# First batch of a Fourier filter and MLP mixer: filter requests moved to an earlier stage and to one queue, its real part doubled on chip, mixer input read in two parts

## The chip, the cores and the metric

The kernel runs on one core of a Trainium2 chip. The metric is the device time of one execution in microseconds (us). Executions of one program mostly agree within 0.3%. A "ratio" below is the mean time of one kernel's fast runs over that of the other's of the same rounds, so it is not quite the ratio of the medians quoted beside it. Where one run's profile is compared with another's, the times are those of the profiled execution.

## The reference

A filter in the frequency domain, then an MLP mixer, all float32 apart from the 64-bit weights.

```python
# x: (8, 3008, 256); filt_r, filt_i: (1505, 256)
X = np.fft.rfft(x, axis=1)
y = np.fft.irfft(X * (filt_r + 1j * filt_i)[None], n=3008, axis=1).astype(np.float32)
xt = y.transpose(0, 2, 1)
h  = np.maximum(xt @ w_tok1, 0.0) @ w_tok2        # token MLP, 256 hidden, 64-bit weights
u  = y + h.transpose(0, 2, 1)
out = (u + np.maximum(u @ w_ch1, 0.0) @ w_ch2).astype(np.float32)   # channel MLP, 1536 hidden
```

## The kernel before

The transform of length 3008 = 64 x 47 is done as matmuls in two stages. The length-64 stage reads x, multiplies, and stores the result z in HBM (`z_tmp`). The filter stage goes through 32 "residues", in 16 pairs: it reads a pair's rows of z, multiplies them with a table `wb` on TensorE, multiplies the result with the filter on VectorE (three products a residue), transforms back on TensorE, lets ScalarE copy the result out of the accumulator into a buffer `t3`, and stores it in HBM as g (`g_tmp`). The mixer then reads g as `t4` in six pieces. Only the first of the five groups of batches does this with no mixer of another batch beside it. During it SP also loads the 64-bit weights w1 and GpSimd w2, and VectorE converts them in `convert()` steps, twelve pieces of w1 and sixteen of w2, the last of them after the filter stage has ended.

What the change and the argument touch, with cuts marked by `# ...`:

```python
def filt_load(c, queues):              # a pair's filter: real part twice (both halves of the rows), imaginary once
    t, k0 = filts[c % FB], c * KC      # FB = 3 buffers
    for q, (src, i, p0) in zip(queues, ((filt_r, 0, 0), (filt_r, 0, HALF), (filt_i, 1, HALF))):
        q.dma_start(t[p0:p0 + A, i], raw(src, k0, [[64 * D, A], [D, KC], [1, D]]))
        # ... two more pieces of 16 and 7 rows
# ...
def load(c):                           # in dft(bs)
    # ... wb of the pair: nc.sync.dma_start(wbs[g], ...)
    filt_load(c, (nc.sync, nc.gpsimd, nc.gpsimd) if first else (nc.sync,) * 3)
    # ... z of the pair: nc.sync.dma_start(t2s[c], z_d ...)
# ...
def bi_unit(k):
    # ... matmuls back; t3 has two buffers; ScalarE copies the accumulator into it
    if r == KC - 1:
        # ...
        nc.scalar.dma_start(g_d[b, ts(c, KC)]..., t3[:, :, i, :])
load(0)
load(1)
yield
yield
for k in range(K2 + 1):
    if k < K2:
        b_unit(k)
        if k % KC == 0 and k // KC + 2 < K2 // KC:
            load(k // KC + 2)
    if k >= 1:
        bi_unit(k - 1)
    yield
# ...
def t4_load(b, c):
    t4[b, c] = t4p.tile([P, TC4, D], FP32, tag="t4", name="t4")
    nc.sync.dma_start(t4[b, c], rows_of(g_d, b)[:, ts(c, TC4), :])
```

`nc.sync` is the queue of SyncE (SP), `nc.gpsimd` that of GpSimd, `nc.scalar` that of ScalarE (ACT). One point of the built program, which the source does not show: the transfers that SP and ACT issue use eight completion counters in turn, and each transfer is issued only once the one eight before it has landed. The traces record it: the transfers of these two queues signal eight semaphores in turn, 100, 101, 110 to 113, 115 and 116.

## Time and profile before

| | kernel before |
|---|---|
| median | 2620.95 us (3 runs, 2620.94 to 2629.69) |
| profiled span | 2619.4 us |
| VectorE's first filter product | 48.24 us |
| from it to the first product of residue 28 | 75.84 us |
| from there to the end of the last w2 conversion | 47.95 us |
| end of the last w2 conversion, when the mixer starts | 172.03 us |
| from there to the end | 2447.4 us |

The marks are read from VectorE's timeline. From the fourth of the forty slices on TensorE is at 90% or more in all but the last, so a microsecond won before 172.03 us is won at the end unless something later takes it back. The lines themselves stand in the prediction.

### The profile page before, as it was taken

What the parts mean: (1) busy time and instruction counts of PE and PEld (TensorE: products, weight loads), DVE (VectorE), ACT (ScalarE), POOL (GpSimd) and SP (SyncE); (2) the same over time, 40 slices, a digit from 0 to 9 for tenths busy, and PEclk for the clock granted to TensorE, in tenths of its full rate; (3) what the DMA queues carried; (4) which work ended last, traced back from release to release, by engine and by line L of the source; (5) the groups of instructions that cost most, each with busy time, mean ns of one, the idle gap of its engine ahead of it and who ended that gap; (6) DMA issues with size and microseconds to landing.
All of it is one profiled execution on the core that took longest, in us unless ns stands there. A gap on an engine that the chain in (4) does not pass through costs nothing.

```text
span 2619.4 us, 31533 instructions
## 1 busy us (share of the span) xinstructions
PE 2513.3 (96%) x10928; PEld 2000.7 (76%) x10928; DVE 1804.4 (69%) x3461; ACT 678.9 (26%) x1325; POOL 519.3 (20%) x951
## 2 busy tenths in 40 slices
PE   6869999999999999999999999999999999999998
PEld 2446666788878777888787777788888888888887
DVE  3787788645666888646567688745678586647676
ACT  2223222222321222213222222212222122212222
POOL 3534111211121111211212111121121121211212
PEclk7879999999999999999999999999999999999999
DMA  8765433312232332202332222211322111100001
GB/s 235 221 192 177 123 111 111 103 42 89 85 100 63 88 89 61 87 9 90 95 101 85 74 82 75 75 33 56 95 77 84 54 46 55 25 9 8 17 10 22
DMA packets 158104, 212.89 MB, mean 81 GB/s; under 512 B 35012, under 2 KB 106383, under 8 KB 157945
## 3 DMA queue, kind: packets, MB, share of 16 engines
q1 hardware_dynamic: 85897, 120.34, 15.7%
q0 software_dynamic: 30656, 39.92, 6.2%
q10 hardware_dynamic: 41392, 50.62, 5.7%
q8 instruction: 86, 1.41, 0.2%
q14 instruction: 73, 0.60, 0.1%
HBM read 135.77 MB, written 74.97 MB: 80 GB/s over the span
## 4 chain that ended last, share of the span: by engine, by line
PE 74%; DVE 14%; issue 2%; ACT 1%; DMA 0%; DVEq 0%; SPq 0%; POOL 0%; ACTq 0%; POOLq 0%
PE ps_po L562 26%; PE ps_pg L528 15%; PE ps_pg L544 11%; PE ps_acc L488 6%; PE ps_acc L471 6%; PE ps_acc L493 3%; DVE t L506 3%; DVE hh L506 3%; PE ps_b L410 3%; PE ps_b L378 2%; PE ps_acc L434 2%; DVE u L506 2%; DVE s L506 1%; DVE p L425 1%; DVE p L424 1%
## 5 line engine op out<-in xcount | busy, mean ns | idle before, releaser
L506 DVE TENSOR_TENSOR hh<-ps_pg,s 128x512 f32<-128x512 f32 (+3 forms) x864 | 482.8, 586 | 643.8 <-ACT s L531 643.2
L607 POOL DMA_DIRECT2D out_dram<-r x757 | 409.8, 550 | 1964.7 <-ACT hh L549 893.9
L549 ACT ACTIVATE hh<-hh 128x512 f32<-128x512 f32 (+1 forms) x576 | 348.0, 621 | 1103.0 <-DVE hh L506 1103.0
L562 PE MATMUL ps_po<-t,wc 128*128 128x256 f32 (+1 forms) x2304 | 535.5, 375 | 3.5 <-DVE t L506 2.2
L562 PEld LDWEIGHTS ps_po<-t,wc 128*128 128x128 f32 x2304 | 434.4, 190 | 127.6 <-issue 50.8
L562 PE MATMUL ps_po<-hh,wc 128*128 128x256 f32 (+1 forms) x1728 | 413.1, 375 | 3.1 <-ACT hh L549 3.1
L528 PE MATMUL ps_pg<-v,wc 128*128 128x256 f32 (+1 forms) x1728 | 414.1, 376 | 1.6 <-DVE v L506 1.6
L562 PEld LDWEIGHTS ps_po<-hh,wc 128*128 128x128 f32 x1728 | 327.4, 190 | 42.4 <-ACT hh L549 5.1
L528 PEld LDWEIGHTS ps_pg<-v,wc 128*128 128x128 f32 x1728 | 327.6, 190 | 41.7 <-DVE v L506 2.3
L544 PE MATMUL ps_pg<-u,wc 128*128 128x256 f32 (+1 forms) x1152 | 294.1, 378 | 9.6 <-DVE hh L506 9.3
L506 DVE TENSOR_TENSOR t<-t,hh 128x256 f32<-128x256 f32 (+1 forms) x576 | 242.9, 422 | 19.8
L544 PEld LDWEIGHTS ps_pg<-u,wc 128*128 128x128 f32 x1152 | 215.3, 190 | 49.2 <-DVE hh L506 22.3
L506 DVE TENSOR_TENSOR s<-ps_pg,hh 128x512 f32<-128x512 f32 (+1 forms) x288 | 196.1, 681 | 30.6 <-DVE hh L506 0.5
L506 DVE TENSOR_TENSOR t<-hh 128x512 f32<-128x512 f32 (+1 forms) x288 | 192.5, 668 | 0.6 <-ACT hh L549 0.6
L488 PE MATMUL ps_acc<-w,h 128*128 128x512 f32 (+1 forms) x384 | 181.7, 596 | 7.7 <-ACT h L477 3.5
L471 PE MATMUL ps_acc<-t,w 128*128 128x256 f32 x768 | 170.3, 384 | 8.0 <-DMA t<-g_tmp 6.7
L528 PE MATMUL ps_pg<-u,wc 128*128 128x256 f32 (+1 forms) x576 | 170.3, 377 | 0.4 <-DVE hh L506 0.4
L471 PEld LDWEIGHTS ps_acc<-t,w 128*128 128x128 f32 x768 | 147.5, 193 | 29.8 <-issue 7.1
L544 PE MATMUL ps_pg<-v,wc 128*128 128x256 f32 (+1 forms) x576 | 168.9, 375 | 0.0
L410 PE MATMUL ps_b<-t,wb 96*128 96x512 f32 (+1 forms) x288 | 130.3, 533 | 31.8 <-DMA t<-z_tmp 17.6
L434 PE MATMUL ps_acc<-p,wb 128*96 128x256 f32 (+1 forms) x384 | 154.7, 497 | 2.4 <-DVE p L423 1.1
L531 ACT COPY s<-ps_pg 128x256 f32<-128x256 f32 (+1 forms) x288 | 106.0, 368 | 152.0 <-PE ps_pg L528 147.4
(71 smaller groups left out, 1954.2 us busy)
## 6 DMA issues: line engine op xcount, KB each, us to landing
z_tmp<-t ACTq DMA_DIRECT2D x96, 256.0 KB
t<-z_tmp SPq DMA_DIRECT2D x128, 192.0 KB
g_tmp<-t ACTq DMA_DIRECT2D x128, 192.0 KB
t<-g_tmp SPq DMA_DIRECT2D x48, 512.0 KB
x<-in_x_dram SPq DMA_DIRECT2D x184, 128.0 KB
out_dram<-r POOLq DMA_DIRECT2D x698, 32.0 KB, 1.8
wb<-wbi_t SPq DMA_DIRECT2D x80, 224.0 KB
filt<-in_filt_r_dram SPq DMA_DIRECT2D x144, 48.0 KB
```

Source lines behind the costliest of these rows:

```text
L410: nc.tensor.matmul(ps, wbs[k // WC][0:KR, k % WC, 0:P], t2s[k // KC][:, k % KC], start=True, stop=True)
L434: nc.tensor.matmul(ps[0:KR], wbs[k // WC][:, k % WC, P:], p, start=(i == 0), stop=(i == len(parts) - 1))
L471: nc.tensor.matmul(acc[:, t, :], w1[:, a, ts(t, P)], t4[b, a // TC4][:, a % TC4, :], start=(a == 0 and t == 0), stop=(a == A - 1 and t == ...
L488: nc.tensor.matmul(ps[:, 0:w], h1[:, t, ts(dh, P)], w2[:, t, ds(m * 512, w)], start=(t == 0), stop=False)
L493: nc.tensor.matmul(ps[:, ds(q * P, n)], t4[b, c][:, r, ts(dh, P)], wai[:, 0:n], start=False, stop=(q == 3))
L506: nc.vector.tensor_tensor(out=out, in0=in0, in1=in1, op=op)
L528: nc.tensor.matmul(ps[:, 0:hw], wc1[:, jp, n, :], mov, start=True, stop=True)
L531: nc.scalar.copy(out=s[:, 0], in_=g[0][:, 0, 0:hw])
L544: nc.tensor.matmul(ps[:, 0:hw], wc1[:, jp, n, :], mov, start=True, stop=True)
L549: nc.scalar.activation(out=hs, in_=hs, func=AF.Relu)
L562: nc.tensor.matmul(po[i][:, j, 0:hw], wc2[:, jp, n, :], mov, start=(jp == 0 and first == 1), stop=(jp == JP - 1 and last == 1))
L607: q.dma_start(rows[g, e, :, ds(h * A + 4 * m, n)], blocks[ts(g, CW), h, e, 0:n])
```

## The change

Its intent is to take waits for transfers out of the first batch, where nothing hides them. It has three parts: (1) the filter of the first batch is asked for by GpSimd alone, its real part once instead of twice, and ScalarE copies that to the other half of the rows; (2) in the first batch, the first two pairs' filter and wb are asked for during the length-64 stage, and in all groups the z rows are asked for before wb; (3) rows 0 to 95 of the first batch's mixer input, which hold residues 0 to 23, are asked for during the last six steps of the filter stage, and the rest after it.

```diff
+LAST_STEP = NXC + 2 + K2
+EARLY_ROWS = 96
-    def filt_load(c, queues):
+    def filt_load(c, first):
         t, k0 = filts[c % FB], c * KC
-        for q, (src, i, p0) in zip(queues, ((filt_r, 0, 0), (filt_r, 0, HALF), (filt_i, 1, HALF))):
+        q = nc.gpsimd if first else nc.sync
+        for src, i, p0 in ((filt_r, 0, 0), (filt_i, 1, HALF)) + (() if first else ((filt_r, 0, HALF),)):
 # ...
+    def filt_double(c):
+        t = filts[c % FB]
+        nc.scalar.copy(out=t[HALF:P, 0], in_=t[0:HALF, 0])
 # ... w_load(c): wb on nc.sync, then filt_load(c, first)
         for i, u in enumerate(todo):             # the length-64 stage
+            if first and i in (5, 8):
+                w_load(i // 6)
 # ...
-        load(0)
-        load(1)
+        for c in range(2):
+            t2_load(c)
+            if not first:
+                w_load(c)
         yield
         yield
+        if first:
+            filt_double(0)
         for k in range(K2 + 1):
             if k < K2:
                 b_unit(k)
                 if k % KC == 0 and k // KC + 2 < K2 // KC:
-                    load(k // KC + 2)
+                    t2_load(k // KC + 2)
+                    w_load(k // KC + 2)
+                if first and k % KC == KC - 1 and k + 1 < K2:
+                    filt_double(k // KC + 1)
 # ...
-    def t4_load(b, c):
+    def t4_load(b, c, lo=0, hi=P):
 # ... in the main loop, from the length-64 stage's end on:
+                if LAST_STEP - 6 <= i < LAST_STEP:
+                    t4_load(0, i - LAST_STEP + 6, 0, EARLY_ROWS)
 # ... after the stage:
-            t4_load(0, c)
+            t4_load(0, c, EARLY_ROWS)
```

## The prediction

> **What bounds the kernel now.** I began with the page's busy table and its forty slices, to see which part of the kernel the change can touch at all.
>
> ```profile
> PE 2513.3 (96%) x10928; PEld 2000.7 (76%) x10928; DVE 1804.4 (69%) x3461; ACT 678.9 (26%) x1325; POOL 519.3 (20%) x951
> ...
> PE   6869999999999999999999999999999999999998
> DVE  3787788645666888646567688745678586647676
> PEclk7879999999999999999999999999999999999999
> ```
>
> A slice is 65.5 us. TensorE is full from the fourth slice on, so after the first batch's filter nothing but less TensorE work would help, and the change removes none: the built programs of both kernels have the same matmuls in the same order, and the same VectorE list. What can be won lies in the first three slices. In the timeline the first matmul of the mixer proper (L528) starts at 181.10 us. Two per cent of 2620.95 is 52 us, and no reordering takes 52 of these 181 us away, as the sums below show; so the answer is "within 2%" from the start, and the question is how many microseconds.
>
> Next I read the same stretch in the timeline of each engine: the length-64 stage is 0 to 38 us, the filter stage (L410 to L439) 47 to 134 us, the mixer's weights, token sums and first inputs up to 181 us. Windows over the last two (first line: columns):
>
> ```profile
> core 0: us, PE busy (x) PEld busy (x) DVE busy (x) ACT busy (x) POOL busy (x), PEclk, DMA share, GB/s
> 48.20:133.10 84.90, 71.94 (x234) 41.84 (x232) 65.70 (x145) 23.86 (x53) 48.07 (x87) 0.91 0.78 214
> 133.10:172.00 38.90, 26.51 (x101) 20.83 (x101) 36.97 (x85) 9.77 (x18) 13.25 (x25) 0.80 0.80 255
> ```
>
> From 133 to 172 us VectorE is busy 37.0 of 38.9 us, and the rest is the few hundredths between instructions: it converts the weights w2 without a pause. The end of that stretch shows who waits for whom:
>
> ```profile
> 140.51 23.76 PE L471 MATMUL ps_acc<-t,w 128*128 128x256 f32 x96 [6.74 <-DMA t<-g_tmp]
> 167.78 2.07 PE L488 MATMUL ps_acc<-w,h 128*128 128x512 f32 x2 [3.51 <-ACT h L477]
> 172.00 2.08 PE L488 MATMUL ps_acc<-w,h 128*128 128x512 f32 x2 [2.14 <-DVE w L242]
> ...
> 171.17 0.86 DVE L242 TENSOR_TENSOR w<-both 128x368 f32<-128x368 f32 x2
> ```
>
> TensorE waits 6.74 us for the mixer input, but its token sums are ready at 164.3 us and their relu at 167.7 us; what starts the mixer at 172.0 us is VectorE's last w2 conversion. So VectorE carries the path from the filter stage's end, and a gain must shorten the filter stage as VectorE sees it. There VectorE is busy 65.7 of 84.9 us. The gaps that its timeline lists there (larger than the 0.03 us between any two) add up to 0.78 + 2.83 + 1.25 + 0.71 + 0.20 + 1.68 + 4.06 + 1.44 + 0.20 + 1.64 + 0.94 = 15.7 us. They start at TensorE, which waits for the z rows:
>
> ```profile
> 68.10 1.19 PE L410 MATMUL ps_b<-t,wb 96*128 96x256 f32 x2 [2.70 <-DMA t<-z_tmp]
> 69.08 1.91 PE L434 MATMUL ps_acc<-p,wb 128*96 128x256 f32 x4
> ...
> 96.46 1.22 PE L410 MATMUL ps_b<-t,wb 96*128 96x256 f32 x2 [3.41 <-DMA t<-z_tmp]
> ```
>
> and those rows come late because their request stands in the SP queue behind other things. The waits of that queue from 38 to 137 us:
>
> ```profile
> SPq L401 <- PE ps_acc L434: 21.3, 11, 3.9
> SPq L465 <- DMA g_tmp<-t: 15.0, 2, 7.8
> SPq L193 <- DMA g_tmp<-t: 9.0, 2, 5.0
> SPq L406 <- DMA g_tmp<-t: 6.6, 2, 4.8
> ```
>
> L401 (the table wb) waits 21.3 us for a free buffer, with the z request behind it. L193 and L406 (filter, z) wait 15.6 us for g_tmp, which they don't read: in the built program the transfers of SP and ACT share eight completion counters in turn, so each waits for the one eight before it. With wb, three filter pieces and z, one store of g and 1.33 w1 pieces for two residues (7.3 transfers), eight back is the previous pair's g store, just issued.
>
> **The Trainium skill.** "DMA: Bandwidth & Descriptors", section "Anatomy of one DMA": most of a transfer's fixed time is the receipt of the write, heaviest when the target is HBM. This trace agrees: the stores of g are what the SP queue waits for, up to 5.0 us at L193. Its "Rules for kernel authors" say that several issuing queues save only issue time, as the same 16 engines move all; so giving the filter to GpSimd wins no bandwidth, and only the bytes dropped count. "TensorE: Matmul & The Clock Gate", section "What's actually happening": after an idle window of about 3.4 us the array runs at half clock until it has been busy as long. Here too: the four-instruction group L434 takes 1.91 us at 69.08 and 1.03 us at 76.08; so a z wait costs again after it (the gaps of 1.25, 0.71 and 1.44 us). "ScalarE: Activation LUTs", section "What ACT_TABLE_LOAD costs": 186 ns + 0.833 ns per column, 613 ns for 512; L256's copies of 512 columns took 0.59 us.
>
> **The change part by part.**
> Removed: SP's 3 filter pieces for each pair of residues, of 24 + 23 rows of two 1 KB packets. That is 15 x 94 = 1410 packets in the filter stage, 55 ns each on the trace (mean of that queue's 1 KB packets), over 16 engines 4.8 us of 0.78 x 84.9 = 66 us of DMA time. GpSimd issues as many pieces as before; its first three groups are asked for by 14.2 us in both kernels, since nothing in its queue holds them.
> Moved: the z request ahead of wb, so it no longer waits for L434 or the filter. Per pair 4.3 transfers on the eight counters instead of 7.3, so eight back is nearly two pairs old, some 8 us at VectorE's pace, longer than the 5 us seen. I expect the six waits for z (0.78 + 2.83 + 1.68 + 4.06 + 1.64 + 0.94 = 11.9 us of VectorE's gaps) and their half-clock echoes (3.4 us) to go for the greater part.
> VectorE's pace sets what is left: three residues take 9 x 0.445 us for the products and 2.26 us for a w1 conversion, 6.26 us; TensorE needs 6.14 us for the same (75.65 to 81.79), so the two are nearly level and a hiccup of either is paid.
> Added: 16 copies of 64 x 512 on ScalarE, 0.59 us each, 9.4 us of an engine busy 23.9 of 84.9 us. Most fit in its 1.19 us pauses between two evacuations L439. In five of the 16 places (the step after a w1 conversion, an even one) the copy falls between L214 and an evacuation with only 0.13 us free (L214 ends 58.53, L439 starts 58.66), which delays it by 0.45 us; the acc bank is single, so TensorE pays: 5 x 0.45 = 2.3 us. The copies also need the filter's real part a step before VectorE did; GpSimd's pieces land 3.8 us after issue and are asked for some 8 us ahead. I leave 2.5 us for copies or z rows that still come late, with the stage compressed.
> Stage: 15.7 - 2.3 - 2.5 = about 11 us.
> The start: two wb (128 packets of 107 ns each on 16 engines, 0.86 us) go into the length-64 stage, where the DMA share reaches 1.0; that may cost up to 1.7 us. In return z is asked for as soon as the last z store lands (SP waited for that until 43.21 and asked at 44.32): 1.1 us won. Net +0.5 us lost.
> The mixer input in two parts: three quarters arrive before the stage ends, so TensorE's 6.74 us shrink to perhaps 3. All of it is behind VectorE, which already binds by 172.0 - 167.7 = 4.3 us: worth 0.
> The later batches only reorder requests; there L410's waits (14.0 us) are for VectorE, not for transfers: 0.
> Sum: 2620.95 - 11 + 0.5 = 2610.5, say 2611.
>
> **Rivals.** (a) Transfers bind by volume: the stage keeps its DMA-limited length and gains only the 4.8 us removed: 2616. For it: DMA share 0.78 with 1.0 in places; against: 61 us of DMA work fit in 74. (b) The doubling becomes the new wait: ScalarE stands in order behind a late filter, evacuations slip, and 16 x 0.6 us come back: 2620. For it: TensorE and VectorE are level, GpSimd also carries w2 in the second half (landing 5.3 us); against: the pauses of ScalarE. (c) The early mixer input is worth its 3.7 us too, because something ties w2 to it: 2607. Against it: VectorE's unbroken conversions. (d) The start loses more than I think: wb delays the last x, all moves by 3 us: 2613.
>
> **Range and chances.** The stage's gain lies between 4 and 15.7 us, start and rest within 2 us; two of the three times of before agree to 0.01 us, one is 8.7 us off. Range 2603 to 2619. Faster or slower by 2% needs 52 us either way: 0.01 each.
>
> **What would show it.** In the changed profile: the waits of L410 for z under 5 us in all; the span from VectorE's first product to its last under 76 us (84.8 before); copies of 0.59 us and few evacuations waiting behind them; VectorE still without pauses up to the last w2 conversion, now near 161 us, and TensorE still waiting for it; the token sums' wait shorter without effect. I am wrong if the z waits stay, if ScalarE waits for the filter by microseconds, or if w2's end moves by a different amount than the last product.

## The result, and the profile after

The changed kernel took 2618.26 us (median of 4 runs, 2615.93 to 2619.16), the kernel before 2621.26 us in the same rounds (4 runs, 2620.94 to 2629.69): ratio 0.9979, with a 95% interval of 0.9959 to 1.0. The range and the class "within 2%" held, but the range by 0.7 us only, and one of the four runs (2619.16 us, the profiled one) lies above it; the centre, 2611 us, was 7 us too low. The profile says which terms of the sum were wrong. First its page (busy table and slices):

```profile
PE 2510.9 (96%) x10928; PEld 2000.0 (76%) x10928; DVE 1804.1 (69%) x3461; ACT 688.5 (26%) x1341; POOL 518.9 (20%) x951
...
PE   5869999999999999999999999999999999999998
DVE  3887788646666788646567788745678586647676
...
PEclk7989999999999999999999999999999999999999
```

The work is what it was; ScalarE alone has 16 instructions and 9.6 us more, which are the copies. Only the first three slices can differ, so the same marks are compared:

| us | first product | to residue 28 | to end of w2 | w2 ends | rest | span |
|---|---|---|---|---|---|---|
| before | 48.24 | 75.84 | 47.95 | 172.03 | 2447.4 | 2619.4 |
| changed | 50.83 | 62.57 | 54.32 | 167.72 | 2449.7 | 2617.4 |
| difference | +2.59 | -13.27 | +6.37 | -4.31 | +2.3 | -2.0 |

So the stage up to residue 28 gained 13.3 us, as much as was hoped for; the start lost 2.6 us, and the stretch behind residue 28 lost 6.4 us. The mixer starts 4.3 us earlier, and 2.3 us of that do not reach the end of this profiled run: TensorE had two more half-clock stretches after the mixer's start (near 204 and 870 us) than the kernel before. A repeat of the changed kernel (e0 below) had neither and a rest of 2446.6 us, so this is variation between runs and not the change.

The windows of the changed kernel (columns as in the prediction's windows: stretch, its length, busy time of TensorE, weight loads, VectorE, ScalarE and GpSimd, granted clock, DMA share, GB/s):

```profile
50.80:113.00 62.20, 59.04 (x207) 34.57 (x207) 57.14 (x125) 29.76 (x61) 47.45 (x85) 0.98 0.87 237
113.00:131.00 18.00, 10.42 (x28) 5.36 (x26) 10.78 (x26) 3.68 (x9) 1.61 (x3) 0.83 0.90 260
131.00:168.00 37.00, 24.79 (x99) 20.00 (x100) 34.63 (x79) 9.29 (x17) 12.51 (x24) 0.82 0.67 185
```

Up to 113 us VectorE and TensorE are both above 90% busy and the clock is 0.98; in the kernel before it was 0.91 over the whole stage. Then come 18 us in which VectorE is busy only 10.8, with the DMA share at 0.90, the highest of the three.

The waits of the SP queue from 38 to 140 us (line, what it waited for: total us, times, longest):

```profile
SPq L401 <- PE ps_acc L448: 34.0, 13, 3.7
SPq L487 <- DMA g_tmp<-t: 18.6, 1, 18.6
SPq L420 <- PE ps_pg L424: 8.6, 5, 4.4
SPq L420 <- DMA z_tmp<-t: 7.0, 1, 7.0
```

The waits of z and filter for g stores (L406 and L193 before) are gone. What is left for g_tmp is L487, the second part of the mixer input, which really needs the last g store. The 7.0 us for z_tmp are the first z request, before the stage.

TensorE's timeline (start, duration, instruction; in brackets the idle time before it and what ended it):

```profile
49.54 1.19 PE L424 MATMUL ps_b<-t,wb 96*128 96x256 f32 x2 [9.05 <-DMA t<-z_tmp]
...
135.47 22.40 PE L493 MATMUL ps_acc<-t,w 128*128 128x256 f32 x96 [5.31 <-DMA t<-g_tmp]
...
163.52 2.07 PE L510 MATMUL ps_acc<-w,h 128*128 128x512 f32 x2 [5.65 <-ACT h L499]
...
167.69 2.08 PE L510 MATMUL ps_acc<-w,h 128*128 128x512 f32 x2 [2.10 <-DVE w L250]
```

The wait of 9.05 us for z is the one that opens the stage; inside it no wait for z is left. At the end the mixer still starts on VectorE's last w2 conversion (L250), so a loss on VectorE's path is a loss in the time.

The loss itself stands in the timelines of ScalarE and VectorE. ScalarE:

```profile
113.83 0.31 ACTq L458 DMA_DIRECT2D g_tmp<-t  x1
115.75 0.62 ACT L202 COPY filt<-filt 64x512 f32<-64x512 f32 x1 [1.95 <-DMA filt<-in_filt_r_dram]
117.19 0.37 ACT L453 COPY t<-ps_acc 96x256 f32<-96x256 f32 x1 [0.82 <-DMA g_tmp<-t]
...
127.72 0.37 ACT L453 COPY t<-ps_acc 96x256 f32<-96x256 f32 x1 [4.51 <-DMA g_tmp<-t]
```

VectorE:

```profile
119.73 0.43 DVE L438 SCALAR_TENSOR_TENSOR p<-ps_b,filt 64x256 f32<-64x256 f32 x1 [2.91 <-DMA filt<-in_filt_i_dram]
...
131.58 0.36 DVE L224 TENSOR_SCALAR both<-both 128x376 uint32<-128x376 uint32 x1 [4.03 <-ACT both L222]
```

L453 writes a `t3` buffer, of which there are two, and each waits for the store that last used it. The store issued at 113.83 us is the one that the evacuation at 127.72 us waits for, so it took about 13.9 us; the one issued at 109.26 us held the evacuation at 117.19 us, some 7.9 us. The evacuation at 127.72 us stands in ScalarE's order before the step of the w2 conversion that is ScalarE's (L222), and so VectorE stands idle for 4.03 us although the weight itself has nothing to do with g. The filter pieces come late too: 1.95 us ahead of a copy, 2.91 us ahead of a product. SP had asked for the first early part of the mixer input at 109.38 us.

### The profile page after: what moved, and what is told of

Read it like the earlier page. It is cut to its first block, busy times and chain, and to the rows that moved or that the text cites. A ratio compares the mean times of both kernels' runs of the same rounds, so it can differ in the third digit from the quotient of the medians.

```text
span 2617.4 us, 31439 instructions
## 1 busy us (share of the span) xinstructions
PE 2510.9 (96%) x10928; PEld 2000.0 (76%) x10928; DVE 1804.1 (69%) x3461; ACT 688.5 (26%) x1341; POOL 518.9 (20%) x951
## 4 chain that ended last, share of the span: by engine, by line
PE 74%; DVE 14%; issue 2%; ACT 1%; DMA 1%; DVEq 0%; SPq 0%; POOL 0%; ACTq 0%; POOLq 0%
PE ps_po L584 26%; PE ps_pg L550 15%; PE ps_pg L566 11%; PE ps_acc L510 6%; PE ps_acc L493 6%; PE ps_acc L515 3%; DVE hh L528 3%; DVE t L528 3%; PE ps_b L424 3%; PE ps_b L386 2%; PE ps_acc L448 2%; DVE u L528 2%; DVE s L528 2%; DVE p L439 1%; DVE p L438 1%
## 5 line engine op out<-in xcount | busy, mean ns | idle before, releaser
L448 PE MATMUL ps_acc<-p,wb 128*96 128x256 f32 (+1 forms) x384 | 154.5, 496 | 10.5 <-ACT t L453 8.6
```

The lines of the kernel that those rows point to most:

```text
L448: nc.tensor.matmul(ps[0:KR], wbs[k // WC][:, k % WC, P:], p, start=(i == 0), stop=(i == len(parts) - 1))
```

## The experiments

The theory after the result: the gain comes from the filter's transfers that no longer stand among the eight counters (and perhaps from z going ahead of wb), and the early read of 2.36 MB (six parts of 384 KB) delays the last g stores and filter pieces. One rival for the lost time (B) was that the shorter stage lets GpSimd's w2 loads, 376 KB each, fall on the last residues whatever the mixer input does. Another (C) was that TensorE's own chain, the token sums, had become the bound, so that the early read could not hurt or help. Nine runs were made. Runs of the kernel before: median 2623.2 us (9 runs) for e1, e2, e4 and e6, 2620.55 us (7 runs) for e0, e3, e5 and e8, and 2624.15 us (7 runs) for e9. All outputs were correct.

| us | first product | to residue 28 | to end of w2 | w2 ends | rest | median | ratio to before |
|---|---|---|---|---|---|---|---|
| e0 changed again | 51.64 | 62.52 | 51.91 | 166.07 | 2446.6 | 2614.66 | 0.9978 [0.9963, 0.9993] |
| e1 one read | 50.28 | 63.54 | 47.05 | 160.87 | 2446.1 | 2608.89 | 0.9947 [0.9935, 0.9960] |
| e2 early read only | 49.35 | 75.16 | 53.07 | 177.58 | 2448.5 | 2625.63 | 1.0010 [0.9997, 1.0024] |
| e6 early read of 48 rows | 48.90 | 62.11 | 50.61 | 161.62 | 2447.2 | 2611.53 | 0.9956 [0.9943, 0.9970] |
| e4 no doubling | 51.86 | 72.85 | 47.24 | 171.95 | 2446.4 | 2619.21 | 0.9986 [0.9971, 1.0002] |
| e3 wb late | 47.44 | 62.27 | 47.00 | 156.71 | 2447.9 | 2608.20 | 0.9953 [0.9938, 0.9968] |
| e5 doubling only | 47.47 | 62.47 | 47.12 | 157.06 | 2448.7 | 2607.16 | 0.9949 [0.9932, 0.9965] |
| e8 early read, 1 KB packets | 47.41 | 62.48 | 51.27 | 161.16 | 2447.3 | 2612.40 | 0.9969 [0.9954, 0.9984] |
| e9 doubling, tiny transfers | 47.31 | 75.35 | 49.68 | 172.34 | 2449.2 | 2623.15 | 0.9991 [0.9968, 1.0014] |

### e1: the mixer input in one read

```diff
-                if LAST_STEP - 6 <= i < LAST_STEP:
-                    t4_load(0, i - LAST_STEP + 6, 0, EARLY_ROWS)
 # ...
-            t4_load(0, c, EARLY_ROWS)
+            t4_load(0, c)
```

> The changed kernel with the mixer input read in one part again, after the last residue. Marks on VectorE's timeline: first product (before 48.2, changed 50.8 us), first product of residue 28 (124.1, 113.4), end of the last w2 conversion (172.0, 167.7); the tail from residue 28 to that end grew from 48.0 to 54.3 us in the changed kernel. Theory A: the early read fills the DMA engines while the last g stores and filter pieces need them. Then the tail falls back to about 48 us, the last w2 conversion ends near 161.4 us, and the time is some 6 us under the changed kernel, about 2612 us. Rival B: the crowd is GpSimd's four w2 loads, which come in a bunch because the stage is faster; then the tail stays at 54 us and the time near 2618 us. Rival C: the later mixer input makes TensorE's token sums the end of the path; then the w2 conversions end near 161 us, but the mixer's first input starts microseconds after that.

The stretch behind residue 28 fell from 54.32 us (51.91 in e0) to 47.05, and the median of the run to 2608.89 us. The same stretch of time as in the changed kernel's second window, and then TensorE's timeline:

```profile
113.00:131.00 18.00, 9.87 (x34) 5.63 (x33) 17.09 (x40) 6.60 (x15) 2.68 (x5) 0.81 0.68 220
```

```profile
129.47 23.42 PE L493 MATMUL ps_acc<-t,w 128*128 128x256 f32 x96 [6.83 <-DMA t<-g_tmp]
...
160.84 2.08 PE L510 MATMUL ps_acc<-w,h 128*128 128x512 f32 x2 [2.10 <-DVE w L250]
```

VectorE is busy 17.1 of the 18 us instead of 10.8, and the DMA share is 0.68 instead of 0.90. ScalarE shows no wait for a g store between 104 and 124 us. Three w2 loads are asked for in a bunch here too, from 111.1 to 113.5 us (111.4 to 113.1 in the changed kernel), but they land in 4.4 to 4.7 us instead of 10.5 to 14.5, so rival B falls. TensorE waits longer for its input than before the removal (6.83 us against 5.31), and still starts the mixer on VectorE's conversion, 6.85 us earlier: rival C falls. The times agree: the ratios to the kernel before of e1 (0.9935 to 0.9960) and of the changed kernel's repeat e0 (0.9963 to 0.9993) do not overlap.

### e2: the early read alone, in the kernel before

```diff
 # kernel before, plus LAST_STEP, EARLY_ROWS and t4_load(b, c, lo, hi)
+                if LAST_STEP - 6 <= i < LAST_STEP:
+                    t4_load(0, i - LAST_STEP + 6, 0, EARLY_ROWS)
 # ...
-            t4_load(0, c)
+            t4_load(0, c, EARLY_ROWS)
```

> The kernel before with only the mixer input read in two parts. Theory A: the same crowding in a slower stage; the tail grows from 48.0 us by 3 to 6 us, the time to 2624 to 2627 us, and the shorter wait of the token sums wins nothing. Rival B (w2 loads): tail 48 us, time 2621 us as before. My prediction's step (the early read is worth 0) would also give 2621 us.

```profile
177.56 2.07 PE L491 MATMUL ps_acc<-w,h 128*128 128x512 f32 x2 [2.11 <-DVE w L244]
```

The stretch behind residue 28 grew by 5.1 us (53.07 against 47.95), and the mixer started 5.6 us later, again on VectorE's conversion. VectorE again had a gap of 4.99 us behind ScalarE's step of the conversion (at 141.51 us). The medians differ by 2.4 us only, and the interval just includes 1, so the time alone would not prove the cost; the trace shows it, and it is there without any other part of the change.

### e6: half the rows early

```diff
-EARLY_ROWS = 96
+EARLY_ROWS = 48
```

> The changed kernel with 48 instead of 96 rows read early (half the bytes, asked at the same places). Theory A: the excess of the tail over 48.0 us halves, from 6.4 to about 3 us; time about 2615 us. Rival B: the tail stays at 54 us. A third theory, that a g store waits on the completion counter of an early read rather than for the engines' bandwidth, would leave the tail nearly as it is, since the number of transfers is unchanged.

The stretch took 50.61 us. Over the 47.05 of e1 that is 3.6 us, where 96 rows cost 4.9 (e0) and 7.3 us (the first profile). Half the bytes cost less, but not clearly half. ScalarE still waited 3.64 us for a g store. The third theory of the expectation, a g store held by the completion counter of an early read, does not apply here: in the changed kernel, e0 and e6 each g store of this stretch was issued within 0.03 us of the end of its evacuation.

### e4: no doubling, the order and the early requests kept

```diff
 # e1, and:
-        for src, i, p0 in ((filt_r, 0, 0), (filt_i, 1, HALF)) + (() if first else ((filt_r, 0, HALF),)):
+        for src, i, p0 in ((filt_r, 0, 0), (filt_i, 1, HALF), (filt_r, 0, HALF)):
+            if first and (i, p0) == (0, HALF):
+                q = nc.sync
 # ... both calls of filt_double removed
```

> As e1_one_read, but no doubling: the real part's second copy is loaded by SP behind wb, as three pieces, the z request still first. It tells what of the 13.3 us won between the first product and residue 28 (75.8 to 62.6 us) is the order of the requests and what is the doubling with its fewer transfers. My prediction's reading (both matter: order frees z from wb's wait, fewer transfers age the eight counters): 66 to 70 us. If order alone is enough: 63 us or less, as ScalarE's copies go too. If the number of transfers on the shared counters is what counts: 72 us or more, with waits of the SP queue for g stores back.

```profile
79.53 1.19 PE L426 MATMUL ps_b<-t,wb 96*128 96x256 f32 x2 [2.93 <-DMA wb<-wbi_t]
```

```profile
81.32 0.43 DVE L439 TENSOR_TENSOR p<-ps_b,filt 128x256 f32<-128x256 f32 x1 [4.10 <-DMA filt<-in_filt_r_dram]
...
99.24 0.42 DVE L439 TENSOR_TENSOR p<-ps_b,filt 128x256 f32<-128x256 f32 x1 [3.64 <-DMA filt<-in_filt_r_dram]
```

The stage to residue 28 took 72.85 us: 10 of the 13 us are gone. Of the outcomes named beforehand it was the third and not the prediction's reading (66 to 70 us), and SP's waits for g stores are back (8.6 us at L403, wb). With z first, the waits did not vanish; they moved to whatever now came last in the queue, wb and the filter's real part. The order is worth 3 us at most when the filter stays on SP.

### e0: the changed kernel again

No edit.

> The changed kernel again, on another chip perhaps, to tell what of its marks repeats. It ended 2449.7 us after its last w2 conversion, the kernel before 2447.4 and e1_one_read 2446.1, with two more half-clock windows on TensorE late in the trace (near 204 and 870 us). If those are chance, that stretch comes to 2446 to 2448 us this time; if they belong to the change, to 2449 us or more. The tail from residue 28 to the last w2 conversion should be about 54 us again (theory A).

The median was 2614.66 us against 2620.55 us for the kernel before, ratio 0.9978. The marks vary: 51.91 us behind residue 28 instead of 54.32, and a rest of 2446.6 us instead of 2449.7. Differences of 2 or 3 us between two single profiles carry no argument here.

### e3: wb asked for late

```diff
 # e1, and wb split off w_load as wb_load:
             if first and i in (5, 8):
-                w_load(i // 6)
+                filt_load(i // 6, first)
 # ...
         for c in range(2):
             t2_load(c)
+            wb_load(c)
             if not first:
-                w_load(c)
+                filt_load(c, first)
```

> As e1_one_read, but the first two wb are asked for behind the z requests, not in the length-64 stage. The first product came at 48.2 us before, at 50.8 and 50.3 us with wb early, but also at 48.9 (wb early) and 49.4 (wb late) in others. If the early wb delays the last z store (my prediction: up to 1.7 us), the first product comes 1 to 2 us sooner than 50.3 us, near 49 us, and the time is 1 to 2 us under e1_one_read. If wb behind z is itself waited for, the first product stays at 50 us or later and nothing is won.

The first product came at 47.44 us instead of 50.28, and the stage was as short as before. Single profiles vary, so all of them are taken: the six kernels with wb in the length-64 stage have first products at 50.83, 51.64, 50.28, 51.86, 48.90 and 47.41 us, on average 50.15; the five others at 48.24, 49.35, 47.44, 47.47 and 47.31 us, on average 47.96. With the early wb the first product is about 2.2 us later on average, but with a spread of 4 us among the six, and the lowest of them (47.41, e8) is as early as the others. The times do not confirm a cost: as ratios to the kernel before, e3 (0.9953) and e5 (0.9949, wb late too) do not differ from e1 (0.9947). It was run at another time. That the early wb costs time is not shown.

### e5: the doubling alone

```diff
 # kernel before, and:
-    for q, (src, i, p0) in zip(queues, ((filt_r, 0, 0), (filt_r, 0, HALF), (filt_i, 1, HALF))):
+    parts = ((filt_r, 0, 0), (filt_i, 1, HALF)) if queues is None else (... the three of before)
+    for q, (src, i, p0) in zip(queues or (nc.gpsimd,) * 2, parts):
 # ...
-    filt_load(c, (nc.sync, nc.gpsimd, nc.gpsimd) if first else (nc.sync,) * 3)
+    filt_load(c, None if first else (nc.sync,) * 3)
 # ... filt_double called where the changed kernel calls it; wb still before z, one read of the mixer input
```

> The kernel before with the doubling alone: SP asks for no filter, but wb still stands before z and is asked for after the length-64 stage. e4_no_double showed that the order alone leaves 72.8 us from the first product to residue 28 (75.8 before, 62.6 to 63.5 with both). If the number of transfers on the eight shared counters is the cause of the waits, the doubling alone brings 63 to 65 us and a time within 3 us of e1_one_read. If z must also be ahead of wb's wait for its buffer, it brings 67 to 71 us, with waits of TensorE for z left.

The waits of its SP queue from 47 to 125 us (a third entry, 0.4 us for the w2 conversion, is not shown):

```profile
SPq L406 <- PE ps_acc L439: 41.8, 13, 7.3
SPq L474 <- DMA g_tmp<-t: 15.0, 3, 8.3
```

The whole gain of the stage is there, 62.47 us to residue 28, although z still stands behind wb, which waits 41.8 us for its free buffer (L406). VectorE's gaps after the first product come to 1.70 us, where the kernel before had 15.7. Only the mixer input (L474) waits for g stores now; neither filter nor z waits for another transfer. The median, 2607.16 us, is the best of all, 7.5 us below the changed kernel.

### e8: the early read in 1 KB packets

```diff
 # changed kernel; the early part of t4_load becomes
+            for h in range(2):
+                nc.sync.dma_start(t4[b, c][lo:hi, h::2], src[:, h::2, :])
```

> The changed kernel with each early read as two transfers of alternate rows: the same bytes in packets of 1 KB instead of 4 KB. If the engines take turns between queues by packets, a g store (1 KB packets) loses less to each turn, and the tail's excess over 48 us falls from 6.4 to 3 to 5 us. If only the bytes count, it stays at 6 us; if the twelve transfers instead of six weigh on the eight counters, it grows.

If the DMA engines took turns between queues by packet, smaller packets of the read should have let the g stores through. The stretch took 51.27 us, against 51.91 in e0 and 54.32 in the first profile: within what two runs of one kernel differ by. The trace says more than this sum, for the wait is another one. ScalarE:

```profile
113.51 0.37 ACT L453 COPY t<-ps_acc 96x256 f32<-96x256 f32 x1 [1.19 <-PE ps_acc L448]
119.91 0.31 ACTq L458 DMA_DIRECT2D g_tmp<-t  x1
120.26 0.58 ACT L264 COPY w<-ps_po 128x512 f32<-128x512 f32 x1 [6.38 <-DMA t<-g_tmp]
```

No evacuation waits for a `t3` buffer any more: the store issued at 110.31 us had nearly all its packets moved from 115 to 118 us, where that of 113.83 us in the changed kernel needed from 118 to 127.7 us. But the next store, due at 113.88 us, was issued only at 119.91 us, when the completion counter that it shares with the early read of 108.29 us came free. The smaller packets may have eased one wait, and the six transfers more brought another; what the packets alone are worth stays open.

### e9: the doubling, with three tiny transfers a pair put back

```diff
 # e5, and in load(c), before the z request:
+    if first:
+        for n in range(3):
+            nc.sync.dma_start(idle[0:A, (3 * c + n) % 16, :], raw(filt_r, c * KC + n, [[64 * D, A], [1, 8]]))
```

> e5_double_only plus three tiny loads (24 rows of 32 bytes, never read) on the SP queue where the three filter pieces stood: the count of transfers is that of the kernel before, the bytes are those of the doubling. The stretch from the first product to residue 28 was 75.8 us before and 62.5 us with the doubling alone. If the count on the eight shared completion counters is the cause, most of the 13.3 us comes back: 70 to 76 us, with waits of the SP queue for g stores and of TensorE for z. If the bytes and packets of the filter pieces are the cause, it stays at 62 to 64 us.

Each of the three brings 24 rows of 32 bytes into a tile that nothing reads: the count of the removed transfers without their bytes. Its SP queue's waits from 47 to 125 us, and TensorE's waits:

```profile
SPq L407 <- PE ps_acc L443: 23.6, 8, 4.6
SPq L411 <- DMA g_tmp<-t: 4.1, 3, 2.2
SPq L407 <- DMA g_tmp<-t: 3.2, 2, 2.9
SPq L407 <- DMA st<-in_moe_w_tok_dram: 1.8, 2, 1.3
```

```profile
75.53 0.70 PE L419 MATMUL ps_b<-t,wb 96*128 96x256 f32 x2 [1.88 <-DMA t<-z_tmp]
...
92.38 0.70 PE L419 MATMUL ps_b<-t,wb 96*128 96x256 f32 x2 [2.34 <-DMA t<-z_tmp]
...
109.81 0.70 PE L419 MATMUL ps_b<-t,wb 96*128 96x256 f32 x2 [2.94 <-DMA t<-z_tmp]
```

The stage is back at 75.35 us (75.84 in the kernel before), and wb (L407) and the tiny loads (L411) wait for g stores that they do not read. All waits of this queue for transfers that the request does not need sum to 14.2 us. So the gain was neither bytes nor order but the number of transfers on the shared counters. Two reservations: the tiny loads also take about 1 us of SP's issue time a pair, and one of the four timed runs was at 2614.28 us where the others lay from 2623.03 to 2626.38 us, which I cannot explain.

## Why the prediction was right or wrong

**The bound, and the class: right.** All of it happened in the first 170 us, the mixer started on VectorE's last w2 conversion in every trace in which I looked at it, and 52 us were out of reach.

**The stage's gain, predicted 11 us from first to last product: right in mechanism, and conservative.** First to last product went from 84.8 to 73.9 us (50.83 to 124.70), under the predicted 76; without the early read it was 71.6 us (e1), a gain of 13.2. The step "4.3 transfers on the eight counters instead of 7.3" is what e5 and e9 confirm: doubling alone gives 62.47 us to residue 28, three tiny transfers a pair give 75.35. The other half of that step, "the z request ahead of wb", is not needed: e5 has the old order and loses nothing. What the prediction held back for copies and late rows, 2.3 and 2.5 us, was about 1.9 us of gaps on VectorE up to residue 28 (0.46 + 0.36 + 0.85 + 0.24). The hiccups are where it put them, at five steps after a conversion, about 0.55 us each on TensorE. The copies took 0.62 us, not the 0.59 of L256; the figures that the prediction takes from "ScalarE: Activation LUTs" are those of an ACTIVATE with immediate scale and bias, and give an estimate of 0.61 us for 512 columns.

**The start, predicted +0.5 us: mis-sized.** It was +2.6 in the profile and about 2.2 on average over the traces. The prediction gave wb up to 1.7 us and took back 1.1 us for an earlier z request. That credit did not come: SP waited for the last z store until 46.60 us, not until 43.21, because the last store of the length-64 stage landed later. That the early wb is what delayed this store was not shown (e3).

**The failed step: "The mixer input in two parts ... worth 0".** This is where the centre was lost. The prediction asked only who waits for the mixer input (TensorE, with slack behind VectorE), and that was right: TensorE's wait shrank from 6.74 to 5.31 us without effect. It did not ask what the early 2.36 MB would delay. They were sent when the last g stores, filter pieces and w2 loads were also under way; the store of 113.83 us kept one of the two `t3` buffers for 13.9 us, ScalarE stood behind it, and with it the w2 conversion that sets the mixer's start. In the changed kernel this cost 4.9 to 7.3 us (e0 and the first profile against e1), in the kernel before 5.1 us (e2). With 5 to 7 us here and 1.7 to 2.1 us at the start, less the 2.2 us more that the stage gave once freed of it (13.2 against 11), the centre of 2611 becomes 2615.5 to 2617.9 us; the two calls gave 2618.26 and 2614.66.

**The rivals of the prediction.** (a) Volume: fell, as e9 gives back nearly the whole gain with 2.3 KB a pair (3 x 24 x 32 bytes). (b) The doubling as a new wait: fell for the stage; one copy waited 1.95 us for its filter at 115.75 us, in the stretch crowded by the early read. (c) The early input is worth 3.7 us: the opposite. (d) A costly start: partly right. That GpSimd's queue brings no bandwidth, which the prediction takes from "Rules for kernel authors", no run here tests.

**Still open.** How the early read holds up the g stores is settled in part. ScalarE's queue moved no data from 116 to 118 us, although the store of 113.83 us was waiting; no run gives a reason. From 118 us on this store shared the engines with the early read and the w2 loads. What each queue moved from 119 to 124 us in the changed kernel (packets, MB, share of the engines' time; q0 is GpSimd's queue, q1 SP's, q10 ScalarE's):

```profile
q0 software_dynamic: 159, 0.76, 50.0%
q1 hardware_dynamic: 169, 0.60, 37.9%
q10 hardware_dynamic: 160, 0.16, 13.3%
```

The three moved nearly the same number of packets, but those of the w2 loads are of about 6 KB, those of the early read of 4 KB and those of the g stores of 1 KB, so the g stores got about a tenth of the bytes. The Trainium skill, in "DMA: Bandwidth & Descriptors", section "Queues, rings and completion order", says that each DMA engine goes round between the queue rows it has work for, a packet at a time. These five microseconds agree with it, and so do those of e0 (172, 176 and 158 packets); e8, where 635 packets of SP's queue went beside 173 of GpSimd's from 110 to 115 us, does not show equal turns. Nor is the spread of 4 us at the start explained.

## What to carry to other kernels

Before a transfer is moved earlier, ask what shares the DMA engines with it at the new time and which buffers those transfers hold: a read that nobody needs yet can delay a store that two buffers depend on. When a queue waits for something that it does not read, count the transfers between the two as well as their bytes; here three small ones fewer per pair gave the whole gain, and cutting a read into more pieces made a store wait (e8). Try the parts of a change singly: of the three here only the doubling was worth keeping, and alone (e5, 2607.16 us) it beats both kernels.

## What the Trainium skill lacked or had wrong

- "DMA: Bandwidth & Descriptors" advises, in the section "Why a DMA increments its semaphore by 16 and not by 1", "One semaphore per in-flight slot, not one per stream." It lacks what a small pool of completion counters, used in turn by two queues, does to unrelated transfers: with three tiny transfers more per pair the stage to residue 28 took 75.35 us instead of 62.47 (e9 against e5).
- The same page, under "Anatomy of one DMA", gives a fixed time and a rate for a transfer. It lacks a measured time of a whole transfer among others on busy engines: at a DMA share of 0.90 a g store of 192 KB was released about 13.9 us after its issue; and the w2 loads of 376 KB landed a median of 8.7 us after issue from 105 to 132 us, where in the kernel before (105 to 140 us) it was 5.3.
- "TensorE: Matmul & The Clock Gate", section "What's actually happening", has the half clock follow an idle window of about 3.4 us, as the prediction cites. Here shorter waits were enough: 2.70 us in the kernel before (granted clock 0.50 from 67.8 to 74.4 us) and 1.88 us in e9 (0.51 from 76.7 to 80.1 us), while no half clock followed the wait of 2.08 us before 85.33 us in the kernel before (1.00 from 75 to 90 us).
